# A Fourier mixing layer with a two-layer product on one core: how the first group of rows is normalised, when its mixture is formed, and when five pieces are folded

## The chip, the cores and the metric

One core of a Trainium2 chip runs the whole program. The metric is the device time of one execution in microseconds (us), and the median of three executions stands for the kernel. Five engines work side by side, each through its own list of instructions in order: PE (TensorE, matmuls), DVE (VectorE), ACT (ScalarE), POOL (GpSimd) and SP (SyncE), which here issues nearly all DMA transfers. An engine that waits for a semaphore holds up everything behind it in its own list.

## What is computed

Input x has 8 batches of 3136 positions and 256 channels.

```python
X = np.fft.rfft(x, axis=1)
y = np.fft.irfft(X * F, n=3136, axis=1)              # F: complex filter, per frequency and channel
mixed = np.real(np.fft.fft(np.fft.fft(y, axis=1), axis=2))
u = y + mixed
un = (u - mean(u)) / np.sqrt(var(u) + 1e-06)         # over the channels
out = u + np.maximum(un @ w_ch1, 0.0) @ w_ch2        # 256 -> 1024 -> 256
```

## The kernel before, in words

**The work.** The forward transform of a batch is two matmul passes (`forward1`, `forward2`), with the filter applied in `spectrum`. From the filtered spectrum two things are made. `inverse1` and `inverse2` give y; between the two the data makes a trip through DRAM (`d2`, stored at L689 and loaded at L736), and y itself goes to DRAM as `dy`. `fold` gives the spectrum's even and odd parts, in seven pieces of 224 slots per batch, as an fp16 high half and a low half in `eo`: POOL adds (L633, L646), ACT writes the high half (L662), DVE the low half (L664). A piece of batch 0 is scaled by `first`, which needs the largest values of x and of the filter (`scale_first`, `prepare_filters`, `pow2`).

**The groups.** The 12544 rows are taken in 49 groups of 256 slots (two tiles of 128). For a group, `prepare` forms the mixture on PE from `eo` (`channels`, L890), adds y to it on DVE (L900), takes mean and variance (L957, L958), the root on ACT (L964), normalises on ACT (L984), splits in fp16 halves (L987 ACT, L999 POOL), and transposes by DMA (L1004). Group 0 differs: y comes straight from `direct` (L763) and was copied from PSUM by ACT (L766), the low half is made by DVE and the transpose is done on PE (`flip`, L313). `first_product` makes for each of eight slices `h_0` to `h_7` six matmuls (L1028), a relu on ACT (L1038) and the low half on DVE (L1039); `second_product` makes twelve matmuls per slice (L1058) and at the end adds on DVE (L1067) and stores.

**Weights.** w1 and w2 come as 64-bit words. `widen` (four DVE operations L1078 to L1084 and one on ACT, L1082) makes fp32 of each quarter, `squares` finds the largest column, `bound_weights` the scale, `split_weights` the fp16 halves (L1153 ACT, L1140 DVE).

**What sets the order.** The main program is a list of steps written by hand: `advance` steps the forward side, `give` steps the way back, `weigh` the weights by tables of step numbers (`WIDEN_AT`, `SQUARE_AT`, `BOUND_AT`). A scheduler then places instructions on each engine, with `after(...)` as further constraints, so the order on an engine is known only from the built program. `warm` puts matmuls on PE whose result nothing reads ("idle" in the rows).

**Batch 1** begins with loads of x (`x_0` to `x_6`, L449), seven squares on ACT (`xsq`, L455), the scale `sx`, and then its first pass (`s_1_0` and on, L479), whose table `s1f` is loaded on SP's queue at L477 behind the transposes L1004.

```python
for _ in range(AHEAD):
    next(work, None)               # group 1 begins ahead of the product loop
...
warm(34, "i1", p=idle[0])          # L678
...
if b == 0 and c < 8:
    warm(6, "i2", p=idle[0])       # L809, behind each of y_2 to y_7
```

## Time and profile before

| | |
|---|---|
| median of 3 executions | 1445.79 us (1441.25 to 1446.78) |
| the profiled execution, its own time | 1446.62 us |
| span of the profiled execution | 1444.8 us |
| busy: PE, DVE, ACT, POOL | 1403.2 (97%), 1045.3 (72%), 757.8 (52%), 507.4 (35%) us |
| the two products, L1058 and L1028 | 592.7 and 581.4 us busy on PE |
| chain that ended last, shares by engine | PE 64%, DVE 12%, DMA 10%, issue 6% |
| granted TensorE clock, mean | 0.996 |

How to read it: the span runs from the first to the last instruction, and the 1.8 us between it and the execution's time lie around it. Busy shares are averages over the whole span. In the rows further down a line of a timeline gives start, duration, engine, line, operation, output and inputs, shapes, how many were merged, and in brackets the idle time ahead of it with what ended it. Merged or neighbouring instructions overlap a little, so the step from one to the next is often 0.05 to 0.1 us shorter than the duration of one.

### The profile page before, as it was taken

What the parts mean: (1) busy time and instruction counts of PE and PEld (TensorE: products, weight loads), DVE (VectorE), ACT (ScalarE), POOL (GpSimd) and SP (SyncE); (2) the same over time, 40 slices, a digit from 0 to 9 for tenths busy, and PEclk for the clock granted to TensorE, in tenths of its full rate; (3) what the DMA queues carried; (4) which work ended last, traced back from release to release, by engine and by line L of the source; (5) the groups of instructions that cost most, each with busy time, mean ns of one, the idle gap of its engine ahead of it and who ended that gap; (6) DMA issues with size and microseconds to landing.
All of it is one profiled execution on the core that took longest, in us unless ns stands there. A gap on an engine that the chain in (4) does not pass through costs nothing.

```text
span 1444.8 us, 30052 instructions
## 1 busy us (share of the span) xinstructions
PE 1403.2 (97%) x11292; PEld 948.3 (66%) x11292; DVE 1045.3 (72%) x2326; ACT 757.8 (52%) x1418; POOL 507.4 (35%) x641
## 2 busy tenths in 40 slices
PE   9988999899999999999999999999999999999998
PEld 8745676467666676666766776666766667666666
DVE  7885793679797777978678876987768876545553
ACT  6666455546465554745546554565447564444341
POOL 2521581068103840157300871048400673011010
PEclk9999999999999999999999999999999999999999
DMA  9667888689857967589566987589575987452320
GB/s 361 228 210 204 220 193 243 191 219 227 262 153 184 230 175 245 162 205 226 155 225 178 242 193 208 157 233 245 137 257 155 222 191 196 109 156 80 88 59 29
DMA packets 434221, 276.42 MB, mean 191 GB/s; under 512 B 218796, under 2 KB 401084, under 8 KB 434076
## 3 DMA queue, kind: packets, MB, share of 16 engines
q1 hardware_dynamic: 433948, 274.47, 70.4%
q8 instruction: 88, 1.44, 0.4%
q14 instruction: 57, 0.47, 0.1%
q10 hardware_dynamic: 128, 0.05, 0.0%
HBM read 124.41 MB, written 99.17 MB: 155 GB/s over the span
## 4 chain that ended last, share of the span: by engine, by line
PE 64%; DVE 12%; DMA 10%; issue 6%; ACT 3%; POOL 3%; SPq 2%; DVEq 0%; ACTq 0%; POOLq 0%
PE h L1028 24%; PE acc L1058 23%; DMA x<-x 2%; PE y L801 2%; DVE y L900 2%; PE s L493 2%; DMA at<-d 2%; PE mix L890 2%; DVE h L1039 2%; DMA d<-ast 2%; PE s L479 1%; PE s L590 1%; PE i L684 1%; PE i L686 1%; PE i L685 1%
## 5 line engine op out<-in xcount | busy, mean ns | idle before, releaser
L1028 PE MATMUL h<-ut,home 128*128 128x512 f16 x2352 | 581.4, 380 | 15.2 <-DVE h L1039 7.6
L1058 PE MATMUL acc<-w2s,h 128*128 128x256 f16 x4704 | 592.7, 273 | 2.4 <-DVE y L1067 1.4
L1058 PEld LDWEIGHTS <-h 128*128 128x128 f16 x4704 | 455.5, 98 | 146.3 <-issue 16.4
L1038 ACT ACTIVATE h<-h 128x512 f16<-128x512 f32 x392 | 233.2, 596 | 374.0 <-PE h L1028 364.9
L1039 DVE SCALAR_TENSOR_TENSOR h<-h,h 128x512 f16<-128x512 f32 x392 | 267.8, 685 | 212.5 <-ACT h L1038 211.4
L1028 PEld LDWEIGHTS <-home 128*128 128x128 f16 x2352 | 221.6, 98 | 226.1 <-issue 37.5
L999 POOL TENSOR_TENSOR u<-un,u 128x512 f16<-128x512 f32 x96 | 110.8, 1171 | 674.7 <-ACT u L987 616.1
L900 DVE SCALAR_TENSOR_TENSOR y<-mix,alpha,y 128x508 f32<-128x508 f32 (+1 forms) x368 | 155.9, 476 | 2.1 <-PE mix L890 1.0
L984 ACT ACTIVATE un<-y,sb 128x256 f32<-128x256 f32 x194 | 101.0, 592 | 39.4 <-DVE sb L973 34.4
L607 POOL TENSOR_TENSOR yt<-yt,t 128x224 f32<-128x224 f32 x108 | 75.6, 700 | 119.5 <-DVE t L599 58.7
L812 ACT ACTIVATE ys<-y,alpha 128x512 f32<-128x512 f32 x98 | 66.7, 687 | 61.3 <-PE y L801 60.8
L688 DVE TENSOR_TENSOR bt<-i,bt 112x512 f16<-112x512 f32 x98 | 66.3, 684 | 43.9 <-ACT bt L687 40.9
L1067 DVE SCALAR_TENSOR_TENSOR y<-acc,beta,y 128x512 f32<-128x512 f32 x98 | 71.0, 745 | 25.8 <-PE acc L1058 25.7
L633 POOL TENSOR_TENSOR ef<-yt 128x224 f32<-128x224 f32 x112 | 73.0, 672 | 35.0 <-PE utt L313 17.5
L621 POOL TENSOR_TENSOR home<-yt,home 128x448 f16<-128x448 f32 x77 | 79.5, 1036 | 11.6 <-ACT home L620 11.5
L595 DVE SCALAR_TENSOR_TENSOR yt<-s,pF,ft 128x448 f32<-128x448 f32 x98 | 66.0, 675 | 24.2 <-PE s L591 17.5
L687 ACT CAST bt<-i 112x512 f16<-112x512 f32 x98 | 56.8, 584 | 48.6 <-PE i L686 42.4
L608 POOL TENSOR_TENSOR yt<-yt,t 128x224 f32<-128x224 f32 x108 | 73.1, 679 | 0.0
L957 DVE BATCH_NORM_STATS2 st<-y 128x6 f32<-128x256 f32 x196 | 72.9, 411 | 0.2
L306 DVE TENSOR_REDUCE mx<-x 112x1 f32<-112x1024 f32 x42 | 51.0, 1215 | 25.6 <-DMA x<-x 25.4
L599 DVE SCALAR_TENSOR_TENSOR t<-s,pF,ft 128x448 f32<-128x448 f32 x98 | 66.1, 675 | 0.6 <-POOL yt L608 0.6
L659 POOL TENSOR_TENSOR eo<-ef,eo 128x448 f16<-128x448 f32 (+6 forms) x55 | 51.6, 942 | 33.8 <-ACT eo L658 32.4
(168 smaller groups left out, 1662.0 us busy)
## 6 DMA issues: line engine op xcount, KB each, us to landing
x<-x SPq DMA_DIRECT2D x55, 512.0 KB
out<-y SPq DMA_DIRECT2D x98, 256.0 KB
at<-d SPq DMA_DIRECT2D x49, 512.0 KB
b<-d SPq DMA_DIRECT2D x49, 512.0 KB
dy<-ys SPq DMA_DIRECT2D x206, 112.0 KB
y<-dy SPq DMA_DIRECT2D x90, 256.0 KB
d<-ast SPq DMA_DIRECT2D x98, 224.0 KB
d<-bt SPq DMA_DIRECT2D x98, 224.0 KB
```

Source lines behind the costliest of these rows:

```text
L607: nc.gpsimd.tensor_tensor(yh[:, 0], yh[:, 0], t2v[:, 1], op=ALU.subtract)
L608: marks["sum"] = nc.gpsimd.tensor_tensor(yh[:, 1], yh[:, 1], t2v[:, 0], op=ALU.add).ins
L621: nc.gpsimd.tensor_tensor(ylo, ytv, yhi, op=ALU.subtract)
L633: nc.gpsimd.tensor_tensor(ef[:, i], yt[:, 0, i], yt[:, 1, i], op=o)
L900: nc.vector.scalar_tensor_tensor(out, p, al, y, op0=ALU.mult, op1=ALU.add)
L957: nc.vector.bn_stats(st[:m, 2 * t + k], y[:m, t, k])
L984: nc.scalar.activation(un[:m, k], y[:m, t, k], AF.Identity, bias=sb[:m, i, 1:2], scale=sb[:m, i, 3:4])
L999: marks["u16", g] = low.tensor_tensor(u16[:m, :, :, 1], unv, u16[:m, :, :, 0], op=ALU.subtract).ins
L1028: marks["pe"] = nc.tensor.matmul(p[:, c0 : c0 + n].rearrange("p (t k q) -> p t k q", k=2, q=m), homes["w1s"][:, d, hw, 128 * f : 128 * f + ...
L1038: marks["relu"] = nc.scalar.activation(h[:, 0, :nt], p[:, :nt], AF.Relu).ins
L1039: marks["h"] = nc.vector.scalar_tensor_tensor(h[:, 1, :nt], p[:, :nt], 0.0, h[:, 0, :nt], op0=ALU.max, op1=ALU.subtract).ins
L1058: nc.tensor.matmul(acc[:m, k], h[:, hh, c0 : c0 + m], w2s[:, f, hw], start=f == 0 and k == 0 and i == 0, stop=f == 7 and k == 1 and i == 2,)
```

## The change

Five things change together.

1. **Scales.** `scale_x` finds the scale of x at step 20 instead of with the filter's at step 50; the filter's squares move from steps 42 to 48 to steps 36 to 42, and `scale_first` to step 49. `first` is formed ahead of `set_alpha`, and the small ACT operation for `fnyqs` goes behind group 0.
2. **Mixture of group 0.** `mixture(0)` is issued ahead of `inverse2`'s first step, so on PE it stands ahead of `direct`. ACT copies it from PSUM to two SBUF tiles, `near` and `point`.
3. **Group 0 by tiles.** `prepare_first` adds y from `direct`'s PSUM bank (`sums[t]`) and takes roots, scales and normalisation per tile. The copy L766 of y is gone.
4. **Folds.** Pieces 0 and 1 of batch 0 are folded as before. Pieces 2 to 6 are folded behind group 0 (`late_fold`), pieces 2 and 3 ahead of the loop, the others at its steps 4 to 6. Their `ef` tiles take buffers of tag `t2`. Group 1's `prepare` is begun inside the loop's first step.
5. **Weights and warming.** Squares are spread over steps 44 to 68, w2's split is started at the loop's step 0 instead of 2, w2's scale is found in group 0's time (step 70 instead of 1001), and `warm` shrinks from 34 to 18 and from 6 to 4.

```diff
-WIDEN_AT = (31, 33, 37, 41, 54, 54, 56, 56)
-SQUARE_AT = (56, 70)
-BOUND_AT = (57, 1001)
+WIDEN_AT = (31, 33, 37, 41, 50, 51, 61, 61)
+SQUARE_AT = (44, 46, 56, 56, 68, 68, 68, 68)
+BOUND_AT = (57, 70)
...
-    def scale_first():
+    def scale_x():
...
         pow2(mx0[:, 7:8], "x0", sx, spare)
         sxs[0] = sx
+
+    def scale_first():
         prepare_filters()
+        marks["first"] = nc.vector.tensor_tensor(first, sxs[0][:, 1:2], pF[:, 1:2], op=ALU.mult).ins
         set_alpha(0)
-        nc.vector.tensor_tensor(first, sx[:, 1:2], pF[:, 1:2], op=ALU.mult)
...
-                    with after("utt", "w2s", "relu"):
+                    with after("utt", "w2s", "relu", ("cast", 1)):
                         nc.scalar.activation(junk, x, AF.Square, accum_out=m[:, k : k + 1])
...
-                        with after("spread" if ch < 4 else "utt"):
+                        with after("spread", "utt", "w2s"):
                             nc.scalar.activation(hi, e, AF.Copy, scale=first)
-                        with after(("u16", 0)):
+                        with after("utc", "w2l"):
                             nc.vector.scalar_tensor_tensor(lo, e, first, hi, op0=ALU.mult, op1=ALU.subtract)
...
-                    warm(34, "i1", p=idle[0])
+                    warm(18, "i1", ("pb", "F"), p=idle[0])
...
-        for ch in range(7) if b == 0 else ():
-            fold(ch)
-            yield
+        if b == 0:
+            for ch in range(2):
+                fold(ch)
+                yield
+            folded.extend(range(2, 7))
+            fold_of.append(fold)
...
-            marks["y0"] = nc.scalar.copy(ys_of[0][:, t], p).ins
+            sums[t] = p
...
-                warm(6, "i2", p=idle[0])
+                warm(4, "i2", p=idle[0])
...
+    def prepare_first():
+
+        pm, fix = mixtures.pop(0)
+        near, point = (fp.tile([128, 2, 256], F32, tag="ast", name=n, bufs=4) for n in ("near", "point"))
+        nc.scalar.copy(near, pm)
+        marks["near"] = nc.scalar.copy(point[:1, 0], fix[0][2]).ins
...
+        for t in range(2):
+            add(y[:, t], pm[:, t], al, sums[t])
...
+            moments(0, y, [(t, groups[0][t])], st, mv)
+            roots(sb, mv, [(128, slice(2 * t, 2 * t + 2))])
+            yield
...
-    while done[0] < 60:
+    while done[0] < 58:
...
-        for q in {28: (0, 4), 29: (2,), 30: (6,), 42: (1,), 44: (5,), 46: (3,), 48: (7,)}.get(n, ()):
+        for q in {28: (0, 4), 29: (2,), 30: (6,), 36: (1,), 38: (5,), 40: (3,), 42: (7,)}.get(n, ()):
             measure_filters(q)
-        if n == 50:
+        if n == 20:
+            scale_x()
+        if n == 49:
             scale_first()
...
+    for _ in mixture(0):
+        pass
+    first_group = prepare_first()
+    next(first_group)
...
+    late_fold()
+    late_fold()
...
-        if q == 1:
-            weigh(1001)
-        if 1 < q < 6:
-            split_weights("w2", q - 2)
+        if q == 0:
+            work = prepare(1)
+            for _ in range(AHEAD):
+                next(work, None)
+        if q < 4:
+            split_weights("w2", q)
+        else:
+            late_fold()
```

Where instructions come to stand, at three places.

DVE, from the scaled maximum of the filter to `first`. Before (`lines_F` itself is eleven rows ahead; `cv`, `home` and `y_3` rows are the widening of w2):

```order
L1084 SCALAR_TENSOR_TENSOR home<-size_777,home 128x512
L1079 SCALAR_TENSOR_TENSOR y_3_582<-raw_739,cv_7_834 128x512
L300 TENSOR_REDUCE pF<-pb_F 128x1
L1080 SCALAR_TENSOR_TENSOR home<-raw_663,home 128x512
L1080 SCALAR_TENSOR_TENSOR y_3_582<-raw_739,y_3_582 128x512
L302 TENSOR_SCALAR pF<-pF 128x1
L1084 SCALAR_TENSOR_TENSOR home<-size_831,home 128x512
L1084 SCALAR_TENSOR_TENSOR y_3_582<-size_838,y_3_582 128x512
L303 TENSOR_SCALAR pF<-pF 128x1
L430 TENSOR_TENSOR first<-sx_714,pF 128x1
```

Now, the whole piece from `lines_F`:

```order
L296 TENSOR_SCALAR lines_F<-ident,mF 128x128
L1128 TENSOR_SCALAR cv_4_745<-raw_598 128x512
L647 MEMSET ef_0_818 128x1
L1129 SCALAR_TENSOR_TENSOR home<-raw_598,cv_4_745 128x512
L1130 SCALAR_TENSOR_TENSOR home<-raw_598,home 128x512
L1134 SCALAR_TENSOR_TENSOR home<-size_749,home 128x512
L300 TENSOR_REDUCE pF<-pb_F 128x1
L302 TENSOR_SCALAR pF<-pF 128x1
L303 TENSOR_SCALAR pF<-pF 128x1
L431 TENSOR_TENSOR first<-sx_271,pF 128x1
```

Of the sixteen widening operations for w2 all stood ahead of `first`; now four do.

ACT, in group 0's product (`h_0_4`, `h_0_6` are relus of slices 4 and 6, `un_0` and `un_1` the normalised tiles of group 1 and then of group 2, `u_1_0` a cast of group 1, `sb` a root, `xsq` the squares of batch 1). Before:

```order
L1038 ACTIVATE h_0_4_1289<-h_4_1282 128x512
L1153 ACTIVATE w2s<-home,sw_1216 128x2x256
L455 ACTIVATE xsq_0_1310,mx_1123<-x_0_1116 112x1024
L455 ACTIVATE xsq_1_1313,mx_1123<-x_1_1117 112x1024
L455 ACTIVATE xsq_2_1316,mx_1123<-x_2_1118 112x1024
L984 ACTIVATE un_0_1173<-y_1127,sb_1166 128x256 x2
L984 ACTIVATE un_1_1190<-y_1127,sb_1166 128x256 x2
L814 COPY ys_10_1305<-y_10_1306 112x512
```

Now:

```order
L1088 ACTIVATE h_0_6_1342<-h_6_1335 128x512
L959 ACTIVATE sb_1311<-mv_1309,eps 128x4
L1049 ACTIVATE un_0_1153<-y_1085,sb_1138 128x256 x2
L1049 ACTIVATE un_1_1162<-y_1085,sb_1138 128x256 x2
L1052 CAST u_1_0_1156<-un_0_1153 128x4x128
L1052 CAST u_1_1_1165<-un_1_1162 128x4x128
L457 ACTIVATE xsq_0_1283,mx_1081<-x_0_1074 112x1024
L457 ACTIVATE xsq_1_1286,mx_1081<-x_1_1075 112x1024
L457 ACTIVATE xsq_2_1289,mx_1081<-x_2_1076 112x1024
L1049 ACTIVATE un_0_1397<-y_1173,sb_1311 128x256 x2
L457 ACTIVATE xsq_3_1329,mx_1081<-x_3_1077 112x1024
L1049 ACTIVATE un_1_1447<-y_1173,sb_1311 128x256 x2
```

Group 1's normalisation and all seven squares now stand behind the relu of slice 6 and behind group 2's root (`sb_1311`). The rows that follow are `xsq_4`, `xsq_5`, the cast of group 2's first tile, `xsq_6`, the cast of its second, and the relu of group 1's slice 0.

SP's queue, around the table `s1f` of batch 1 (`ut_1155` and `ut_1336` are the transposes of groups 1 and 2; `ut_1135` and `ut_1308` now). Before:

```order
L1004 DMA_TRANSPOSE ut_1155<-u_1_0_1176 128x8x128
L1004 DMA_TRANSPOSE ut_1155<-u_1_1_1193 128x8x128
L518 DMA s_1243<-c_s 128x896
L477 DMA s1f_1391<-c_s1f 112x112
L518 DMA s_1243<-c_s 128x896
L1004 DMA_TRANSPOSE ut_1336<-u_2_0_1422 128x8x128
```

Now:

```order
L1054 DMA_TRANSPOSE ut_1135<-u_1_0_1156 128x8x128
L1054 DMA_TRANSPOSE ut_1135<-u_1_1_1165 128x8x128
L1054 DMA_TRANSPOSE ut_1308<-u_2_0_1400 128x8x128
L479 DMA s1f_1369<-c_s1f 112x112
L520 DMA s_1207<-c_s 128x896
```

The load of `s1f` now stands behind group 2's first transpose as well. On PE, ahead of `s_1_0` stand now two slices of group 1 (`h_0` and `h_1`) where there was one, and the second of them takes the PSUM bank of the first, so it waits for that slice's low half on DVE.

## Rows read from the trace of the kernel before

**Rows 1.** Windows: stretch, length, busy us of PE, PEld, DVE, ACT, POOL, then clock, DMA share.

```profile
0.00:100.00 100.00, 90.57 (x605) 67.77 (x606) 78.23 (x184) 63.69 (x130) 34.63 (x49) 1.00 0.78 273
...
300.00:1300.00 1000.00, 986.34 (x8229) 665.86 (x8228) 761.54 (x1668) 532.73 (x990) 395.45 (x499) 1.00 0.76 197
```

**Rows 2.** Timeline of DVE, 53 to 67 us.

```profile
53.87 0.84 DVE L605 TENSOR_TENSOR yt<-yt,t 128x224 f32<-128x224 f32 x1
...
58.30 1.29 DVE L1079 SCALAR_TENSOR_TENSOR home<-raw,cv 128x512 int32<-128x512 int32 x2
...
63.79 0.29 DVE L300 TENSOR_REDUCE pF<-pb_F 128x1 f32<-128x128 f32 x1
...
66.52 0.16 DVE L430 TENSOR_TENSOR first<-sx,pF 128x1 f32<-128x1 f32 x1
```

**Rows 3.** Timeline of ACT at 59 us.

```profile
59.15 0.59 ACT L679 COPY bt<-i 112x512 f32<-112x512 f32 x1 [0.28 <-PE i L673]
```

**Rows 4.** Timeline of PE, 62 to 92 us.

```profile
62.20 4.26 PE L283 MATMUL idle<-still 128*128 128x512 bf16 x19
66.30 5.34 PE L763 MATMUL y<-b,direct 112*128 112x256 f32 x24
...
72.59 0.50 PE L890 MATMUL mix<-mix,eo 128*128 128x129 f16 x7
...
76.27 1.02 PE L791 MATMUL y<-b,i2f 112*112 112x512 f32 x2
...
77.13 1.46 PE L283 MATMUL idle<-still 128*128 128x512 bf16 x6
...
90.19 0.94 PE L313 MATMUL utt<-ident,u 128*128 128x128 f16 x14
...
91.94 1.47 PE L1028 MATMUL h<-ut,home 128*128 128x512 f16 x6 [0.59 <-DVE ut L315]
```

**Rows 5.** Timeline of SP's queue, 62 to 88 us.

```profile
62.36 4.14 SPq L736 DMA_DIRECT2D b<-d_f  x6
...
83.42 1.81 SPq L741 DMA_DIRECT2D dy<-ys  x4
...
87.71 0.39 SPq L877 DMA_DIRECT2D y<-dy  x1
```

**Rows 6.** Timeline of DVE, 91 to 111 us.

```profile
91.80 0.74 DVE L900 SCALAR_TENSOR_TENSOR y<-mix,alpha,y 128x508 f32<-128x508 f32 x1
...
92.98 1.64 DVE L900 SCALAR_TENSOR_TENSOR y<-mix,alpha,y 128x254 f32<-128x254 f32 x4
...
110.21 0.30 DVE L958 BATCH_NORM_AGGREGATE mv<-st 128x2 f32<-128x6 f32 x2
```

**Rows 7.** Timeline of ACT, 104 to 116 us, and of POOL at 115.76 us.

```profile
104.81 1.05 ACT L455 ACTIVATE xsq<-x 112x1024 bf16<-112x1024 f32 x1
...
107.94 2.06 ACT L984 ACTIVATE un<-y,sb 128x256 f32<-128x256 f32 x4
...
115.06 0.63 ACT L987 CAST u<-un 128x512 f16<-128x512 f32 x1
...
115.76 2.28 POOL L999 TENSOR_TENSOR u<-un,u 128x512 f16<-128x512 f32 x2 [15.80 <-ACT u L987]
```

**Rows 8.** Timeline of SP's queue, 117 to 122 us, and of PE behind it.

```profile
117.66 2.69 SPq L1004 DMA_TRANSPOSE ut<-u  x2
...
121.09 0.36 SPq L477 DMA_DIRECT2D s1f<-c_s1f  x1
...
123.63 3.66 PE L479 MATMUL s<-x,s1f 112*112 112x512 f32 x8 [0.18 <-DMA s1f<-c_s1f]
```

**Rows 9.** Windows of one microsecond, as Rows 1; then PE's timeline at 290 us.

```profile
120.00:121.00 1.00, 0.00 (x0) 0.00 (x0) 0.41 (x4) 1.00 (x3) 0.00 (x0) 1.00 0.80 184
...
289.00:290.00 1.00, 0.00 (x0) 0.00 (x0) 1.00 (x3) 0.00 (x0) 0.00 (x0) 0.50 0.97 255
...
290.08 4.81 PE L1028 MATMUL h<-ut,home 128*128 128x512 f16 x12 [4.21 <-DMA ut<-u]
```

More of the change, by code (lines that the diff above doesn't have):

```diff
@@ L938, in prepare, with moments @@
             yield
[L939 to L954 removed]
+        mixtures[g] = pm, fix
+    mixtures = {}
+    def moments(g, y, tiles, st, mv):
+        for t, (g0, g1) in tiles:
             m = g1 - g0
@@ new lines, in prepare @@
+    def prepare(g):
+        tiles = groups[g]
+        yield from mixture(g)
+        pm, fix = mixtures.pop(g)
+        y = ys_of.pop(g)
+        for t, s, _, _ in fix:
+            keep = mp.tile([128, 2, 256], F32, tag="un", name=f"keep_{g}", bufs=2)[:, 0]
+            nc.scalar.copy(keep[s], y[s, t, 1])
+        for t, (g0, g1) in enumerate(tiles):
+            ps = slice(0, g1 - g0)
+            with after(("u16", 0)) if g == 1 else after("h"):
+                add(y[ps, t], pm[ps, t], alpha_of(g0, g1, f"al_{g}_{t}")[ps], y[ps, t])
+        for t, s, pn, al in fix:
+            add_nyquist(y[s, t, 1], pn, al[s], keep[s])
+        yield
+        ut = mp.tile([128, 2, 8, 128], F16, tag="ut", name=f"ut_{g}", bufs=2)
+        mv, st, sb = small(g)
+        n = tiles[0][1] - tiles[0][0]
+        nt = 2 * len(tiles)
+        moments(g, y, list(enumerate(tiles)), st, mv)
+        parts = [(n, slice(0, nt))]
+        if len(tiles) == 2 and tiles[1][1] - tiles[1][0] != n:
+            parts = [(n, slice(0, 2)), (tiles[1][1] - tiles[1][0], slice(2, 4))]
+        roots(sb, mv, parts)
+        yield
+        scales(g, sb, mv, parts)
+        yield
+        for t, (g0, g1) in enumerate(tiles):
+            m = g1 - g0
@@ L1114, in widen_weights, with square_weights @@
         else:
-            with after("low"):
+            with after("low", "first" if i > 4 else ""):
                 widen(w, words[i], f"{i}")
-    def square_weights(name):
+    def square_weights(i):
+        name = ("w1", "w2")[i // 4]
         ws, m = raws[name]
-        with after("act", "y0"):
-            for i, w in enumerate(ws):
-                squares(m[:, i : i + 1], w, f"{name}_{i}")
+        with after("act", "spread" if i in (2, 3) else "", "near"):
+            squares(m[:, i % 4 : i % 4 + 1], ws[i % 4], f"{name}_{i % 4}")
     def bound_weights(name):
         ws, m = raws[name]
-        with after(("u16", 0)):
+        with after("low"):
             nc.vector.tensor_reduce(m[:, 4:5], m[:, 0:4], axis=AX.X, op=ALU.max)
@@ L1139, in lower_weights @@
         for lo, w, scale, hi in lows:
-            nc.vector.scalar_tensor_tensor(lo, w, scale, hi, op0=ALU.mult, op1=ALU.subtract)
+            lowered[:] = [nc.vector.scalar_tensor_tensor(lo, w, scale, hi, op0=ALU.mult, op1=ALU.subtract).ins]
         lows.clear()
@@ L1184, in give @@
     def give(n):
-        while come[0] < min(n, NB * BACK) and done[0] >= STEPS * (come[0] // BACK + 1) - (1 if come[0] >= BACK else 4):
+        while come[0] < min(n, NB * BACK) and done[0] >= STEPS * (come[0] // BACK + 1) - (1 if come[0] >= BACK else 5):
             next(home)
@@ L1239, in _program @@
         give(come[0] + 1)
-    for i, _ in enumerate(prepare(0)):
+    for i, _ in enumerate(first_group):
         weigh(68 + i)
         give(min(come[0] + 1, KEPT))
-    with after(("u16", 0)):
-        weigh(1000)
+    weigh(1000)
+    with after("utt"):
+        nc.scalar.activation(fnyqs, fnyq, AF.Copy, scale=pF[:, 1:2])
     advance(STEPS + 3)
@@ L1248, in _program, with late_fold @@
     halves = load_halves()
-    work = prepare(1)
-    for _ in range(AHEAD):
-        next(work, None)
+    def late_fold():
+        if folded:
+            fold_of[0](folded.pop(0))
+    late_fold()
+    late_fold()
     per = NS // 32
```

143 lines of the change are left out of this document (69 added, 74 removed).

## The prediction, as put on record

> **What bounds the kernel now.** I read the page first: PE is busy 97% of the span. The windows then say where its 3% are missing: from 300 to 1300 us PE is busy 986 of 1000 us, in the first 100 us only 91 [rows 1]. The lists of all engines are the same again from batch 3 on and nearly so from 130 us, so all that this change can move lies ahead of 130 us. It reaches the end only if PE passes 130 us earlier or later with the same work behind it. I therefore followed the timelines from 53 to 130 us, at each idle stretch asking what ended it.
>
> Ahead of group 0's product PE waits on a chain: the filter's scale gives `first` at 66.5 [rows 2], then the fold and mixture, y_2 to y_7, the flips, and h_0 at 91.94 [rows 4]. At the far end of group 0, PE is idle at 120 us [rows 9] until group 1's transposed tiles land. Then `s_1_0`, the first pass of batch 1, starts at 123.63, released by the load of `s1f` [rows 8]. The question is whether a lead at 92 us survives to 123.
>
> The sum is made against the profiled execution (1446.62 us, 1.8 of it outside the span), which lies 0.83 us above the median, 1445.79. I subtract the difference from the median. A measurement of this kernel tells about 0.5%, or 7.2 us, from no change.
>
> **Scales and the early mixture.** The last value `lines_F` rests on is ready when yt ends, 53.87 + 0.84 = 54.7 [rows 2], and nothing of x's scale stands ahead of it any more. Of sixteen widening operations four are left ahead of `first`, at 0.6 us each (two step 1.2, [rows 2]): 54.7 + 2.4 = 57.1 for the reduction that was at 63.79, then under 1 us of small operations. `first` is there at about 58.1, 8.4 us earlier.
>
> This does not move `direct` by 8.4 us. It waits for the trip through DRAM: the last copy to `bt` was at 59.15 [rows 3], the loads of `b` began at 62.36 [rows 5], and `direct` at 66.30 stood behind the last of 34 warming matmuls, 62.20 + 4.26 less overlap [rows 4]. I take the copy 0.3 us earlier, the loads at 62.0, and the first tile landed at 65.2 (bounds: 64, by the 62.36 and the 1 to 2 us that six loads of 4.14 us leave for the first, and 66.3, no change). The mixture costs PE the 1.6 us from 71.6 (66.30 + 5.34) to 72.59 + 0.50 [rows 4]. It moves into the trip, where PE had only warming work, so I cost it at nothing. Its cover: the two high halves, about the 0.6 of a `bt` copy each [rows 3], end near 62, the low halves 0.6 later, the matmuls at 64. If the trip were shorter than that, its 1.6 us would be back ahead of `direct`. The two copies `near` and `point` stand where the copy L766 stood.
>
> **From `direct` to h_0.** `direct` ends at 65.2 + 5.3 = 70.5. y_2 to y_7 cost PE 0.86 each (76.27 to 77.13) and six warms stepped 1.3 us, 0.216 each [rows 4]; with four it is 6 x (0.86 + 0.86) = 10.4, to 80.9. `pb_w` of w2's scale stands behind y_7 on PE, and DVE's reduction of it stands ahead of group 0's low halves, so these come at 81.6 to 82.9. From the last flips to h_0 it was 90.19 to 91.94, or 1.75 us. h_0 at 84.6, **7.3 us earlier**. Of this the 28 warms left out are 28 x 0.216 = 6.0 us. The y halves that DVE adds straight from PSUM and the root taken per tile lie beside y_2 to y_7 and cost nothing there.
>
> **Where the lead goes.** Behind slice 6's relu ACT's list now holds group 2's root, then group 1's normalisation. The root waits for DVE's `mv` of group 2. DVE's list up to there took 91.80 to 110.5 [rows 6], 18.7 us. Now two low halves of folds, two of slices and one of w2s join it, 5 x 0.6 = 3.0 (at a widening operation's price), and 2.0 go, my estimate for the small operations of w2's scale (0.15 to 0.3 each) and half a us idle. It starts at 86.7 (group 1's first add, 5.1 us earlier rather than 7.3 because ACT first copies `ut` and three y and writes the next fold's half). 86.7 + 18.7 + 3.0 - 2.0 = 106.4; the root ends at 106.7.
>
> ACT then runs a closed row [rows 7]: four `un` 2.0, two casts 1.1, three squares 3.1, two `un` 1.0, a square 1.05, two `un` 1.0, two squares 2.1, a cast 0.5: 118.5. POOL's low half takes 1.14 (119.6), SP's transpose about 1.25 (120.9), and `s1f` now stands behind this transpose on SP's queue. From its issue to `s_1_0` it was 121.09 to 123.63, 2.54 us [rows 8]: **`s_1_0` at 123.5, where it was 123.63.** The lead is gone, apart from one slice more that PE has behind it, 1.4 us.
>
> PE's idle time shows where. Group 1's first tiles are cast at 109.2; low half and transposes (117.66 to 122.0, the h ahead of `s_1_0` [rows 8]) put its h_0 at 115. Group 0's work is used up at 109 to 111. Its h_1 shares the PSUM bank and waits for h_0's low half, whose relu stands behind the last square and cast on ACT (120.1): 121.3. So PE is idle from about 110 to 115 and from 116.4 to 121.3.
>
> **The clock.** In the idle microsecond at 120 the granted clock was 1.00; in the one at 289, late in an idle time of 4.21 us, it was 0.50, and the twelve matmuls behind it took 4.81 us where six take 1.47 [rows 4, 9]. So a stretch at the lower level cost about 1.9 us there. The new idle stretches are as long as the one at 290, so I take a drop, at 1.2 us, since part of the slow slice ends before `s1f` lands (bounds: 0 and 1.9). [...]
>
> **Sum:** -1.4 + 1.2 = -0.2 us: 1445.79 - 0.2 = **1445.6 us**. The forecast's own range is 1442.5 to 1448.5: the landing of `b` and the estimates on DVE and ACT give 1 to 2 us either way, the clock 0.7 up and 1.2 down.
>
> **Edits that I cost at nothing.** Folds 2 to 6 leave ACT and DVE ahead of h_0 and stand beside group 0's product; their cover is PE's own work on group 0, from h_0 to the idle time before 120 us, and they are late only for group 1's mixtures (their low halves are among the 3.0 above). w2's split comes two steps earlier; its one operation ahead of group 2's root is among the 3.0 too. w2's squares lie in ACT's gaps while PE is at y_2 to y_7.
>
> **Rivals.**
> *A. The lead is kept whole.* If group 2's `mv` is ready much earlier than 106 us, as when the DVE list is shorter than I count, ACT's row starts at once and `s1f` lands by 116. Then 1445.8 - 7.3 = 1438.5. For it: the squares stood ahead of the normalisation before (104.81 against 107.94, [rows 7]) and the first transposes would come early. Against: the order puts group 2's root ahead of group 1's `un`. Chance 0.10.
> *A2. Part is kept,* 2 to 6 us, about 1442: some of DVE's 18.7 us were waits, or the queue lets `s1f` go earlier. Chance 0.13.
> *B. Slower: y of group 1 comes late.* Its second fetch waits for stores of ys, and the copy of ys_4 stands now behind that of `ut` on ACT (about 85). First store to fetch was 83.42 to 87.71, 4.3 us [rows 5]: issue at 89.2. Before, its landing came no later than the second tile's first add, the last of the four at 92.98, which ends at 94.6 and takes 0.74, so at 93.9 [rows 6]: at most 6.2 us. It would land by 95.4 at the worst, and DVE wants it at 92.1. It decides if it lands after 92.1, that is over 2.9 us from its issue. DVE then stands 3.3 us, group 2's fetch behind three loads of x up to 2 us more, and everything down the closed row moves with it: -1.4 + 3.4 + 2.1 = +4.1, 1449.9. For it: DVE and ACT have no slack from 87 to 120. Against: the transfer is small and 6.2 is only a bound. [...] Chance 0.10.
> *C. The change does not do what it says:* the mixture or y_7 is late and h_0 comes less than 3 us earlier. Then ACT's closed row starts up to 4 us later, and the time is about 1448. Chance 0.05.
>
> **How the numbers follow.** Forecast 0.62, A 0.10, A2 0.13, B 0.10, C 0.05. Faster by over 0.5% (below 1438.6) is A: 0.10. Slower by over 0.5% (above 1453.0) is half of B, with a clock drop more, and a little of C: 0.06. The rest, 0.84, is within it. The range reaches from A, 1438.5, to B's price and a clock drop of 1.6, 1451.5; what B and C have beyond, and what lies below A, is under 2 in 10.
>
> **What would show it.** Right: the reduction of pF at 57 and `first` at 58; the mixture's matmuls ahead of `direct`; h_0 near 84.6; root of group 2 on ACT near 106.7 behind DVE's `mv`; PE idle near 110 to 115 (ended by `ut`) and 116 to 121 (ended by the low half of h); `s_1_0` near 123.5 to 124 behind `s1f`; a granted clock of 0.50 about there; no difference behind 300 us. Wrong: `s_1_0` before 118 (A), an idle DVE at 92 to 95 behind a DMA of y (B), or h_0 after 89 (C).

## The result and the profile after

The change made the kernel **slower**: 1458.45 us, the median of 9 runs (1454.63 to 1460.74), against 1446.78 us (1441.25 to 1451.68) for the kernel before in the same session. The ratio is 1.0072, with an interval of 1.0051 to 1.0092. The forecast was 1445.6 us in a range of 1438.5 to 1451.5, so the range did not hold the time, and the outcome that got a chance of 0.06 came true. A repetition (experiment 5) gave 1.0086.

The profiled execution took 1458.59 us, its span 1456.8. The busy line of the page has the same work in more time:

```profile
PE 1404.8 (96%) x11264; PEld 950.4 (65%) x11264; DVE 1046.5 (72%) x2330; ACT 758.5 (52%) x1419; POOL 508.6 (35%) x641
```

PE is busy 1.6 us longer than before with 28 matmuls less, and idle 10.4 us longer. The windows (stretch, length, busy us of PE, PEld, DVE, ACT, POOL, clock, DMA share) say where; the last line is the kernel before:

```profile
0.00:100.00 100.00, 89.39 (x568) 68.93 (x569) 75.45 (x174) 62.92 (x130) 32.94 (x45) 0.95 0.71 250
70.00:75.00 5.00, 3.43 (x8) 2.83 (x9) 2.88 (x8) 4.14 (x11) 0.00 (x0) 0.57 1.02 344
120.00:130.00 10.00, 2.72 (x6) 0.89 (x7) 0.18 (x2) 10.00 (x22) 2.57 (x3) 0.60 0.25 61
300.00:1300.00 1000.00, 981.70 (x8230) 662.19 (x8229) 763.14 (x1675) 534.16 (x993) 393.71 (x498) 1.00 0.75 197
345.00:500.00 155.00, 145.53 (x1206) 97.89 (x1205) 122.85 (x265) 80.94 (x152) 54.71 (x68) 0.99 0.79 203
...
345.00:500.00 155.00, 151.63 (x1254) 101.94 (x1253) 125.06 (x276) 84.30 (x159) 59.04 (x75) 1.00 0.81 209
```

The first and the fourth line answer to [rows 1]. The second and the third show two places with a lower clock, at 70 and at 120 us (a third, at 46 us, is told in experiment 5). The forecast had "no difference behind 300 us". There is one: 4.6 us of PE's busy time are missing there (986.34 to 981.70). Between 345 and 500 us alone it is 6.1 (151.63 to 145.53), so all of it is lost there, and a little comes back elsewhere.

PE's timeline from 60 us to batch 1 (start, duration, engine, line, operation, output and inputs, in brackets the idle time ahead and what ended it) answers to [rows 4] and [rows 8]:

```profile
60.15 0.22 PE L299 MATMUL pb_F<-lines_F,still 128*128 128x128 bf16 x1 [0.62 <-DVE lines_F L296]
...
62.11 4.05 PE L283 MATMUL idle<-still 128*128 128x512 bf16 x18
66.80 0.29 PE L896 MATMUL mix<-mix,eo 128*128 128x129 f16 x2 [0.64 <-ACT eo L664]
...
71.57 8.37 PE L768 MATMUL y<-b,direct 112*128 112x256 f32 x24 [2.94 <-issue]
79.78 1.02 PE L796 MATMUL y<-b,i2f 112*112 112x512 f32 x2
...
90.13 0.22 PE L299 MATMUL pb_w<-lines_w,still 128*128 128x128 bf16 x1
...
93.53 1.47 PE L1078 MATMUL h<-ut,home 128*128 128x512 f16 x6 [0.79 <-DVE ut L315]
...
124.24 2.72 PE L1078 MATMUL h<-ut,home 128*128 128x512 f16 x6 [5.97 <-DMA ut<-u]
130.72 2.72 PE L1078 MATMUL h<-ut,home 128*128 128x512 f16 x6 [3.77 <-DVE h L1089]
133.33 4.76 PE L481 MATMUL s<-x,s1f 112*112 112x512 f32 x8
```

The mixture stands ahead of `direct`, as the change says. But `direct` starts at 71.57 instead of 66.30 and takes 8.37 us instead of 5.34: the same 24 matmuls, most of them at the lower clock (granted 0.50 from 71 to 77.5). h_0 comes at 93.53, 1.6 us **later** than before, and `s_1_0` at 133.33, 9.7 later. In the repetition h_0 comes at 91.58, a little earlier than before, and `s_1_0` at 132.98 all the same.

Why `direct` is late stands in ACT's timeline. Before, the last copy to `bt` began at 59.15 [rows 3]:

```profile
59.17 0.59 ACT L681 COPY bt<-i 112x512 f32<-112x512 f32 x1 [0.28 <-PE i L675]
...
63.33 0.67 ACT L1132 ACTIVATE size<-raw 128x512 f32<-128x512 f32 x1 [3.08 <-DVE home L1134]
63.90 1.05 ACT L681 COPY bt<-i 112x512 f32<-112x512 f32 x2
```

In the kernel before the next `size` stood behind the last copy, and waited there without harm:

```profile
62.10 0.68 ACT L1082 ACTIVATE size<-raw 128x512 f32<-128x512 f32 x1 [2.36 <-DVE home L1084]
```

In the change `size`, an operation of w2's widening, stands in ACT's list ahead of the last two copies. It waits 3.08 us for DVE, and the copies wait behind it and end at 64.95 (PE's sums for them were done at about 62.2). SP's queue then carries that on ([rows 5] had 62.36):

```profile
67.83 2.60 SPq L743 DMA_DIRECT2D b<-d_f  x5
```

From that issue to `direct` it is 3.74 us; before it was 3.94. And DVE, for which `size` waits, is itself late:

```profile
57.41 0.85 DVE L607 TENSOR_TENSOR yt<-yt,t 128x224 f32<-128x224 f32 x1
58.18 1.92 DVE L296 TENSOR_SCALAR lines_F<-ident,mF 128x128 bf16<-128x128 f32 x1
...
61.19 1.03 DVE L1130 SCALAR_TENSOR_TENSOR home<-raw,home 128x512 int32<-128x512 int32 x1
62.26 1.03 DVE L1134 SCALAR_TENSOR_TENSOR home<-size,home 128x512 f32<-128x512 f32 x1
...
63.79 0.15 DVE L431 TENSOR_TENSOR first<-sx,pF 128x1 f32<-128x1 f32 x1
```

`yt` ends at 58.3 where [rows 2] had 54.7; `lines_F` takes 1.92 us (0.287 in the trace of before), and `pb_F`, which waits for it, now stands on PE ahead of the last eight matmuls that these copies need (PE idles 0.62 us there, above); `first` comes at 63.79, 2.7 us earlier instead of the 8.4 forecast. POOL's timeline has its folds at the same time:

```profile
57.97 0.80 POOL L648 TENSOR_TENSOR ef<-yt 1x224 f32<-1x224 f32 x1
58.74 1.27 POOL L635 TENSOR_TENSOR ef<-yt 128x224 f32<-128x224 f32 x2
```

They end at 60.01, and `lines_F` at 60.10.

Behind h_0 the closed row on ACT is there. Its root starts at 115.82 behind DVE, and the four `un` of group 1 follow:

```profile
115.82 0.30 ACT L959 ACTIVATE sb<-mv,eps 128x4 f32<-128x4 f32 x1 [1.71 <-DVE sb L968]
```

### The profile page after: what moved, and what is told of

Same layout as the page of the kernel before. It is cut to its first block, busy times and chain, and to the rows that moved or that the text cites. A ratio compares the mean times of both kernels' runs of the same rounds, so it can differ in the third digit from the quotient of the medians.

```text
span 1456.8 us, 29996 instructions
## 1 busy us (share of the span) xinstructions
PE 1404.8 (96%) x11264; PEld 950.4 (65%) x11264; DVE 1046.5 (72%) x2330; ACT 758.5 (52%) x1419; POOL 508.6 (35%) x641
## 4 chain that ended last, share of the span: by engine, by line
PE 74%; DMA 9%; issue 5%; DVE 5%; POOL 4%; ACT 2%; SPq 1%; DVEq 0%; POOLq 0%; ACTq 0%
PE h L1078 28%; PE acc L1108 27%; PE s L495 3%; PE y L806 3%; PE mix L896 2%; DMA x<-x 1%; PE i L686 1%; PE s L481 1%; DMA b<-d 1%; DMA at<-d 1%; PE i L688 1%; PE i L687 1%; PE s L592 1%; DMA dy<-ys 1%; PE s L593 1%
## 5 line engine op out<-in xcount | busy, mean ns | idle before, releaser
L1078 PE MATMUL h<-ut,home 128*128 128x512 f16 x2352 | 585.0, 382 | 23.9 <-DMA ut<-u 12.4
L906 DVE SCALAR_TENSOR_TENSOR y<-mix,alpha,y 128x508 f32<-128x508 f32 (+1 forms) x360 | 152.6, 475 | 5.6 <-PE mix L896 4.5
L690 DVE TENSOR_TENSOR bt<-i,bt 112x512 f16<-112x512 f32 x98 | 66.3, 683 | 39.3 <-ACT bt L689 35.0
```

Source lines behind the costliest of these rows:

```text
L906: nc.vector.scalar_tensor_tensor(out, p, al, y, op0=ALU.mult, op1=ALU.add)
L1078: marks["pe"] = nc.tensor.matmul(p[:, c0 : c0 + n].rearrange("p (t k q) -> p t k q", k=2, q=m), homes["w1s"][:, d, hw, 128 * f : 128 * f + ...
```

## Experiments

Each was timed against the kernel before on the same chip, in several executions except where the text says otherwise. Medians of the kernel before lay between 1447.58 and 1448.8 us.

**1. `size` behind the copies of bt.** One edit to the changed kernel:

```diff
-        nc.scalar.activation(size, high.bitcast(F32), AF.Abs)
+        with after("spread" if name in ("6", "7") else ""):
+            nc.scalar.activation(size, high.bitcast(F32), AF.Abs)
```

> Edit: the ACT operation `size` of w2's last two quarters is kept behind the last copy to bt; nothing else of the change differs. Theory T1 (the late start of group 0 comes from ACT: `size` stands ahead of the last two copies to bt and waits for a DVE operation that ends at 63.3, so the trip through DRAM starts about 2.2 us late, PE idles 2.9 us ahead of direct and runs it at the lower clock): last copy to bt ends near 62.5 instead of 64.95, direct starts near 69.4 instead of 71.57 and takes 5.3 us instead of 8.4, h_0 near 88.3 instead of 93.53, and since the back of group 0 only passes it on, s_1_0 near 128 instead of 133.3; time about 1453. Rival R1 (the trip is late because its matmuls are late and DMA is slow, ACT's order does not matter): direct moves by under 0.5 us, time 1458 as the change.

1449.4 us, ratio 1.0014 (0.9996 to 1.0031). The timeline, rows of ACT, SP's queue and PE:

```profile
61.62 0.58 ACT L681 COPY bt<-i 112x512 f32<-112x512 f32 x1 [0.28 <-PE i L675]
...
64.94 3.98 SPq L743 DMA_DIRECT2D b<-d_f  x6
...
68.66 5.42 PE L768 MATMUL y<-b,direct 112*128 112x256 f32 x24 [0.90 <-PE pb_w L299]
...
129.59 5.20 PE L481 MATMUL s<-x,s1f 112*112 112x512 f32 x8
```

The copies wait for PE alone now, `direct` starts 2.9 us earlier than in the profile above (1.7 than in the repetition), PE idles 0.90 us ahead of it, and `direct` takes 5.42 us at full clock (granted 1.00 from 70 to 75). h_0 comes at 87.99, as expected, `s_1_0` 3.7 us earlier than in the change. The edit brings back some 10 of the 11.7 us, more than the theory had priced; but not all of that is the place of `size`, since this program also has another order on all engines from about 145 to 460 us (behind experiment 12).

**2. 34 warms again.** The loads stay late; only PE's idle time ahead of `direct` is filled.

```diff
-                    warm(18, "i1", ("pb", "F"), p=idle[0])
+                    warm(34, "i1", ("pb", "F"), p=idle[0])
```

> Edit: 34 warming matmuls behind the last inverse pass instead of 18; nothing else differs. T1 (direct takes 8.4 us because PE stood idle for 2.9 us and ran at the lower of its two clocks): PE has warming work until about 69.4, granted clock 1.00 from 70 to 78, direct starts near 71.6 as before and takes 5.3 us, h_0 near 90.5, time about 1455.5. Rival R1: direct is slow for another reason (its operands or weights land late); it still takes 8 us and the time stays 1458.

1448.05 us, ratio 1.0005 (0.999 to 1.0019). PE's timeline:

```profile
69.77 5.42 PE L768 MATMUL y<-b,direct 112*128 112x256 f32 x24 [0.55 <-PE mix L896]
```

and the window from 70 to 75 us, as above:

```profile
70.00:75.00 5.00, 5.00 (x24) 4.40 (x24) 4.49 (x12) 4.54 (x12) 0.00 (x0) 1.00 1.01 342
```

`direct` starts only 0.5 us earlier than in the repetition of the change (experiment 5) and still ends 2.8 earlier; h_0 comes at 87.73 against 91.58. So 16 warming matmuls, 16 x 0.216 = 3.5 us of PE's otherwise idle time, kept the clock at 1.00; leaving them out saved nothing and cost 2.8 us at the end of `direct`. `s_1_0` comes at 127.55. The time fell by 11 us where about 3 were expected; here too the order differs, from about 305 to 460 us.

**3. The squares of x early.** In the change they wait for a cast of group 1, which puts them into ACT's closed row. Here that wait is dropped; the late `direct` stays.

```diff
-                    with after("utt", "w2s", "relu", ("cast", 1)):
+                    with after("utt", "w2s", "relu"):
```

> Edit: batch 1's seven squares no longer wait for group 1's casts on ACT; nothing else differs. In this order the load of s1f stands ahead of all transposes on SP's queue, and s_1_0 ahead of group 1's h_0 on PE. Theory T2 (the lead of group 0 is lost behind it, because squares, group 1's and group 2's normalisation form one closed row on ACT and s1f stands behind its end): h_0 of group 0 stays at 93.5, s_1_0 moves from 133.3 to about 118 to 121, PE has no idle stretch over 3 us from 118 to 133 and keeps its clock, time 1446 to 1449. Rival R2 (group 1's tiles are what PE lacks, the squares only fill ACT's idle time): s_1_0 starts no earlier than 129, gain 4 us at most, time 1454 or more.

1445.5 us, ratio 0.9984 (0.9968 to 1.0). `direct` is as bad as in the change (69.78, for 8.52 us) and h_0 at 91.90, yet:

```profile
120.01 6.21 PE L481 MATMUL s<-x,s1f 112*112 112x512 f32 x10 [1.04 <-DMA s1f<-c_s1f]
```

`s_1_0` comes 13 us earlier than in the change from about the same h_0: with the squares the load of `s1f` and `s_1_0` itself move ahead of group 1's products. Behind 160 us this program has the order of the kernel before.

**4. Experiments 1 and 3 together** (both edits as above).

> Edit: both of the two edits, `size` behind the copies to bt and the squares without their wait for group 1's casts. T1 and T2 together: h_0 of group 0 near 88.3, s_1_0 at 113 to 117, time 1440 to 1444, below the kernel before. Rival R3 (the two are not additive, since with s1f early PE waits next for group 1's transposes or for DVE): time 1445 to 1448, as with the squares alone.

1442.94 us, ratio 0.9967 (0.9947 to 0.9986): faster than the kernel before. h_0 at 87.17, `s_1_0` at 115.11. At `s_1_0` the two gains add up (3.7 and 13.3 us alone, 18.2 together). In time they do not: against the repetition of the change they are 9.7 and 13.6 us alone and 16.1 together.

**5. The change once more**, unedited.

> The change itself once more, on the chip and beside the runs of the other kernels of this set, to have its time under the same conditions. T1 and T2: direct at the lower clock in the profile again (over 8 us), h_0 6 to 10 us later than the 84.6 that was forecast, s_1_0 later than 130; time 1455 to 1460. Rival R4 (the first measurement was off by the chip it ran on): time within 3 us of the kernel before.

1459.07 us, ratio 1.0086 (1.0067 to 1.0104). PE's timeline:

```profile
70.31 7.67 PE L768 MATMUL y<-b,direct 112*128 112x256 f32 x24 [2.93 <-issue]
```

and the same window:

```profile
70.00:75.00 5.00, 4.69 (x11) 3.81 (x12) 1.64 (x5) 3.78 (x8) 0.00 (x0) 0.51 0.98 315
```

`s_1_0` is at 132.98 here. Executions differ a little already at 44 us. PE's transposes there, in the kernel before, the profile of the result, this execution and experiment 1:

```profile
43.31 0.65 PE L542 MATMUL at<-ident,xc 128*112 128x128 f32 x4 [0.48 <-ACT at L549]
...
44.16 0.65 PE L544 MATMUL at<-ident,xc 128*112 128x128 f32 x4 [0.48 <-ACT at L551]
...
44.39 0.65 PE L544 MATMUL at<-ident,xc 128*112 128x128 f32 x4 [0.48 <-ACT at L551]
...
44.97 0.65 PE L544 MATMUL at<-ident,xc 128*112 128x128 f32 x4 [0.48 <-ACT at L551]
```

From there to `direct` it is 23.0, 27.4, 25.9 and 23.7 us. The profile of the result had a lower clock at 46 us (0.84 from 40 to 50), which put `direct` 1.5 us later; this execution has not, and the time is the same.

**6. `lines_F` on ACT**, one execution. In experiment 5, as in the change, `lines_F` took 1.92 us on DVE while POOL was in its folds; is it slow of itself, or only there? In the second case the author's estimate was that `direct` would start 1 to 1.5 us earlier. The edit leaves out the floor of 1e-18 for the filter's lines.

```diff
-        nc.vector.tensor_scalar(lines, ident[:rows, :rows], col, 1e-18, op0=ALU.mult, op1=ALU.max)
+        if name == "F":
+            nc.scalar.activation(lines, ident[:rows, :rows], AF.Copy, scale=col)
+        else:
+            nc.vector.tensor_scalar(lines, ident[:rows, :rows], col, 1e-18, op0=ALU.mult, op1=ALU.max)
```

> Edit: the one operation lines_F (the diagonal matrix from the filter's largest value) runs on ACT instead of DVE; its lower bound of 1e-18 is left out. Nothing else of the change differs. [...] Rival R5 (lines_F is slow of itself, or waits for mF): it is as slow on ACT, or its place in time does not change.

1455.37 us, which lies among the times of the change. The timeline, rows of ACT, DVE and POOL:

```profile
55.39 0.40 ACT L297 ACTIVATE lines_F<-ident,mF 128x128 bf16<-128x128 f32 x1
...
56.35 2.12 DVE L1131 TENSOR_SCALAR cv<-raw 128x512 int32<-128x512 int32 x1
...
56.92 1.27 POOL L638 TENSOR_TENSOR ef<-yt 128x224 f32<-128x224 f32 x2
...
61.88 0.42 DVE L1131 TENSOR_SCALAR cv<-raw 128x512 int32<-128x512 int32 x1
```

`lines_F` is quick, but the next operation on DVE now takes 2.12 us, where the same one takes 0.42 later, and ends 0.3 after POOL's folds. The wait moved to another operation; `direct` came 0.3 us earlier once 0.57 are taken off by which this execution ran ahead already at 46 us. That fits POOL's folds as the cause, but the 1 to 1.5 us of the estimate were not there.

**7. The kernel before with the change's warms** (34 to 18 and 6 to 4), nothing else of the change.

> The kernel before with one part of the change alone: 18 warming matmuls instead of 34 and 4 instead of 6. T1 (direct waits for the landing of b, 3.7 us behind the first load at 62.4, and idle time ahead of it costs the clock): direct starts at 66.1 as before, PE idles 2.5 to 4 us ahead of it, and if the granted clock falls direct takes 8 us; y_2 to y_7 save 2.6 us; h_0 between 91 and 94, time within 3 us of the kernel before. Rival R6 (my count: every warming matmul left out is 0.216 us gained): h_0 near 86, lead kept in part, time 1443 to 1446 where the kernel before has 1448.

1448.35 us, ratio 1.0005 (0.999 to 1.0021). PE's timeline:

```profile
67.28 7.11 PE L763 MATMUL y<-b,direct 112*128 112x256 f32 x24 [3.20 <-ACT fnyqs L354]
...
96.31 1.47 PE L1028 MATMUL h<-ut,home 128*128 128x512 f16 x6 [1.32 <-DVE ut L315]
```

With 28 matmuls less h_0 comes 4.4 us **later** than [rows 4]; 1.1 of that this execution was late already at 44 us (44.37), so the matmuls left out make 3.3. `direct` loses its clock about one us in, behind 3.2 us of idle time (granted 0.83 from 65 to 70 and 0.82 from 70 to 75). h_0 is later than the 91 to 94 that were expected. `s_1_0` follows by 3.2 (126.81), the time hardly at all.

**8. Experiment 4, and `s1f` in a buffer of its own**, loaded once and early.

```diff
-                    table = fp.tile([112, 112], F32, tag="x16", name=f"s1f_{b}", bufs=3)
-                    nc.sync.dma_start(table, a["c_s1f"])
+                    if "s1f" not in tables:
+                        tables["s1f"] = cp.tile([112, 112], F32, name="s1f_own")
+                        nc.sync.dma_start(tables["s1f"], a["c_s1f"])
+                    table = tables["s1f"]
```

> The two edits of the fourth run, and s1f has a buffer of its own, so that its load waits for no square. Theory T2 carried on (behind group 0, s_1_0 waits for s1f, whose buffer a square holds until the last part of x lands): s_1_0 starts with the end of group 0's products, near 112 instead of 115.1, PE's idle time of 2.5 us and the lower clock behind it are gone, time 2 to 4 us below the fourth run, 1439 to 1441. Rival R7 (the copies of s_1_0 on ACT need the scale of the last square anyway, PSUM is full after a few products): PE stops after a few matmuls of s_1 until about 117, gain under 1 us.

1441.4 us, ratio 0.9961 (0.9947 to 0.9976), the fastest of all. PE's timeline:

```profile
114.11 0.21 PE L299 MATMUL pb_x<-lines_x,still 112*128 112x112 bf16 x1 [2.28 <-DVE lines_x L296]
114.16 4.50 PE L483 MATMUL s<-x,s1f_own 112*112 112x512 f32 x10
```

Without the load, `s_1_0` waits for DVE's scale of x, and so comes only 1 us earlier than in experiment 4, less than expected. Whether this beats experiment 4 is open: the intervals overlap.

**9. One warm more** (18 to 19), meant to change the scheduler's lists far behind it and nothing that the theories speak of.

> Edit: 19 warming matmuls instead of 18 in the change, nothing else. On PE that is 0.2 us of work in idle time, so by the chip alone it should change nothing. But the scheduler, which places instructions by its own model of time, makes other choices behind it: up to the relu of group 0's slice 5 the lists are those of the change but for a few neighbours, from about 140 us they differ, and they come back to those of the kernel before at about group 9, where the change's own come back at group 11. Theory T4 (of the change's loss some 3 to 5 us arise behind 150 us, from lists of the engines that differ from those of the kernel before, in waits of PE between 340 and 500 us): h_0 and s_1_0 at about the times of the change (91.6 and 133 within 1 us, direct at the lower clock), and yet time 1453 to 1456. Rival R8 (all of it is lost by 133 us and what follows only wanders from execution to execution): time 1457 to 1460, as the change.

1459.25 us, ratio 1.0066 (1.0042 to 1.0091). The expectation took it that the lists differ from about 140 us. The traces show that they do not: ACT, SP and POOL run theirs in the order of the change, PE and DVE with a few neighbours changed ahead of 92 us. So this is the change's order timed once more, with the same time, and it does not tell whether that order costs part of the 12 us.

**10. Group 2's root behind group 1's casts.** It stood at the head of ACT's closed row.

```diff
-        roots(sb, mv, parts)
+        with after(("cast", 1)) if g == 2 else nullcontext():
+            roots(sb, mv, parts)
```

> Edit: the root of group 2 on ACT is queued behind group 1's casts; the squares keep their wait for those casts. Theory T2 (closed row on ACT, in which group 1's normalisation waits for group 2's variance): group 1's un starts behind the relu of slice 6, about 2 us earlier than in the change, group 1's h_0 about 2 us earlier; the load of s1f now stands ahead of group 2's transposes on SP's queue, but its buffer waits for squares, so s_1_0 starts near 128 to 130 instead of 133; by this 1455, and 1450 to 1453 if its other lists behind 150 us are better as well. Rival R9 (the squares alone close the row): group 1's h_0 and s_1_0 within 1 us of the change, time 1457 to 1460.

1455.49 us, ratio 1.0045 (1.003 to 1.0059). Group 1's first product and `s_1_0`:

```profile
122.32 2.72 PE L1079 MATMUL h<-ut,home 128*128 128x512 f16 x6 [5.89 <-DMA ut<-u]
...
130.56 3.85 PE L481 MATMUL s<-x,s1f 112*112 112x512 f32 x8
```

A gain of 3.6 us, to 1455 as expected. Group 1's first product comes 1.9 us earlier and `s_1_0` 2.8: the root's wait is a small part of the row, the squares (experiment 3) the large one. Behind about 300 us this program too has another order than the change.

**11. The kernel before, delayed**: 44 warms more behind y_7, so that h_0 is late; the rest of the text of the program is unchanged.

```diff
-                warm(6, "i2", p=idle[0])
+                warm(50 if c == 7 else 6, "i2", p=idle[0])
```

> The kernel before, with 44 warming matmuls more behind y_7 on PE (9.5 us of work that nothing reads), nothing else: group 0's product begins 9.5 us later, with no idle time of PE ahead of it. It measures what a late group 0 costs at the end of the kernel. Theory T5 (the end follows the start of batch 1's first pass: what is late there by 9 us is late at the end by 9 us or a little more): h_0 near 101.4, s_1_0 near 131 to 133, time 1456 to 1459 where the kernel before has 1448. Rival R10 (what follows has slack, in its waits for DMA at 206 and 290 us, and takes up a part): s_1_0 as late, but time 1451 to 1454; then the change loses the rest elsewhere, behind 133 us.

1453.52 us, ratio 1.0032 (1.0018 to 1.0047). h_0 comes 9.2 us later (101.17), `s_1_0` 4.4 later (128.06), and the time is 5.2 above the kernel before. About half of h_0's lateness is absorbed on the way to batch 1. The time came out as the rival had it, at 1453.5. That the 4.4 us at `s_1_0` and the 5.2 at the end are close does not mean that the delay was passed on, as the table behind experiment 12 shows.

**12. The same with 68 warms more** (`50` is `74`), to see whether a start of batch 1 at 133 us alone makes the loss between 345 and 500 us.

> The kernel before, with 68 warming matmuls more behind y_7 instead of 44 (nothing else of the change). In the profiles so far PE's busy time between 345 and 500 us is 151.0 to 153.2 us where s_1_0 comes at or before 129.6 us, 149.9 where it comes at 130.6, and 145.5 to 146.3 where it comes at 131.5 or later (all three of these with the change's lists). 24 warms more put h_0 at about 106.4 and s_1_0 at about 133.2. T9 (lateness alone: a start of batch 1 behind 131 us uses up the slack of the waits at 350 and 408 us, whatever the lists): PE's busy time in 345 to 500 falls to 145 to 148 us, and the time is 1458 to 1463 us. R9 (those waits are the change's own, by its order of work up to 480 us): the busy time there stays at 150 to 153 us, and the time is 1455.5 to 1458 us, the 4.4 to 5.2 us that s_1_0 comes later than in the shorter delay added to its 1453.5.

1456.77 us, ratio 1.005 (1.0037 to 1.0064), with `s_1_0` at 132.87. The windows, first of this kernel:

```profile
345.00:500.00 155.00, 154.18 (x1269) 104.07 (x1268) 124.62 (x273) 84.18 (x158) 58.16 (x72) 1.00 0.77 207
```

and of experiment 9, with `s_1_0` at 131.55:

```profile
345.00:500.00 155.00, 146.11 (x1218) 97.93 (x1215) 124.42 (x272) 82.31 (x154) 56.89 (x72) 1.00 0.79 203
```

At the same lateness PE loses nothing there in this kernel: lateness alone does not make these waits. They go with the order of work. PE's busy time there is 145.5 to 146.9 us in the change and experiments 5, 6 and 9, which share the change's order, and 149.85 us or more in all others. No run has the change's order with an early `s_1_0`, so whether the order makes the waits without a late start is not shown. What ended the idle time there was, in the change's groups of PE's instructions by line:

```profile
L686 PE MATMUL i<-z,i 112*112 112x256 f16 x22 | 6.4, 291 | 4.5 <-DMA z<-home 3.0 <-DMA z<-y 1.6
L1078 PE MATMUL h<-ut,home 128*128 128x512 f16 x246 | 62.2, 384 | 4.0 <-DVE h L1089 2.0 <-DMA ut<-u 2.0
```

**The order of work, and what becomes of a delay.** A trace holds the instructions of each engine in the order in which they ran, so the orders of two kernels can be compared. One edited operation moves the scheduler's choices far behind it. The change's order differs from that of the kernel before up to about 445 us; experiments 1, 2 and 10, apart from the edit itself, leave the change's order at 145 to 305 us and are back at the old one, but for a neighbour or two, by about 380; experiments 7, 11 and 12 differ from the kernel before up to about 375 as well. The table follows the matmuls of the first product (`h`<-`ut`,`home`), 2352 in every kernel, in the profiled executions: how many us later than in the kernel before the matmul comes that stood there at 270, 453 and 674 us, and the last one.

| kernel | `s_1_0` later by | at 270 | at 453 | at 674 | last |
|---|---|---|---|---|---|
| change | 9.7 | 7.8 | 13.2 | 12.7 | 11.8 |
| 5, the same | 9.4 | 8.1 | 12.4 | 12.7 | 12.7 |
| 9, the same order | 7.9 | 5.9 | 10.3 | 9.6 | 10.8 |
| 6, the same order | 8.0 | 4.8 | 7.8 | 7.5 | 8.6 |
| 10, another order | 6.9 | 5.7 | 7.9 | 6.6 | 7.3 |
| 1, another order | 6.0 | 7.0 | 4.7 | 5.3 | 6.3 |
| 2, another order | 3.9 | 2.7 | 3.0 | 0.7 | 0.2 |
| 7, before, fewer warms | 3.2 | 4.0 | 1.2 | 0.9 | 2.7 |
| 11, before, delayed | 4.4 | 2.8 | 1.0 | 0.6 | 8.2 |
| 12, before, delayed more | 9.2 | 8.2 | 5.7 | 2.5 | 12.8 |

With the change's order a delay grows by 3 to 5 us between 270 and 453 us. With the orders of experiments 1, 7, 11 and 12 it shrinks there by 2 to 3, and with that of 10 it grows by 2. And a late batch 1 is not what 11 and 12 end with: at 674 us they are 0.6 and 2.5 us late, and the rest comes behind that, for a part between 950 and 1100 us (the kernel before, then experiment 12), where the order is the old one; why is open.

```profile
950.00:1100.00 150.00, 147.70 (x1266) 100.43 (x1265) 115.12 (x248) 76.91 (x142) 63.77 (x81) 1.00 0.79 205
...
950.00:1100.00 150.00, 142.99 (x1205) 96.86 (x1204) 106.90 (x232) 71.36 (x134) 64.13 (x82) 0.97 0.77 202
```

## Why the prediction was wrong, point by point

The steps of the sum, beside the profile of the change:

| step | forecast | measured |
|---|---|---|
| `first` | 58.1 | 63.8 |
| last copy to `bt` ends | 59.4 | 64.95 |
| loads of `b` issued | 62.0 | 67.8 |
| `direct` starts | 65.2 | 71.6 |
| `direct` to y_2 | 5.3 | 8.2 |
| y_2 to y_7 | 10.4 | 10.3 |
| y_7 to h_0 | 3.7 | 3.4 |
| h_0 | 84.6 | 93.5 |
| h_0 to group 2's root | 21.8 | 22.3 |
| root to `s_1_0` | 17.1 | 17.5 |
| `s_1_0` | 123.5 | 133.3 |

- **The step that failed** is "I take the copy 0.3 us earlier, the loads at 62.0, and the first tile landed at 65.2". Of its bounds, 64 and 66.3, the upper one was "no change"; a later trip was not among them. The change moves the widening of w2, and with it `size` into ACT's list ahead of two copies of the trip, where it waits for DVE. I counted DVE's widening operations ahead of `first` and did not ask what ACT's list holds ahead of the copies. Of the 8.9 us by which h_0 misses the forecast, 6.4 are this start. By the distances from 44 us (experiment 5) 2.2 of the 6.4 are `size`, which experiment 1 shows by undoing it (25.9 to 23.7). The others are 1.1 that were forecast as a gain and did not come, 0.7 that stay in experiment 1, 0.9 by which the profiled execution was late at 44 us already, and 1.5 of the lower clock at 46 us, which the repetition had not.
- **"It moves into the trip, where PE had only warming work, so I cost it at nothing."** The mixture did fit into the trip. But the warming work that covered the rest was gone with it, and with the trip longer PE stood idle 2.94 us and `direct` ran mostly at the lower clock: 2.9 of the 8.9 us, and experiment 2 gives them back by filling the gap. The prediction asked about the clock at 120 us and not at 70. "Of this the 28 warms left out are 28 x 0.216 = 6.0 us" fails with it: by itself, in the kernel before, leaving them out makes h_0 3.3 us later (experiment 7).
- **"54.7 + 2.4 = 57.1"** for `first` took DVE's durations from a place where POOL did not fold (it was idle from 55.5 to 69.3 us there). `yt`, which stands ahead of `lines_F` in DVE's list, ended 3.6 us later than I read it, and `lines_F` took 1.92 us instead of 0.287. Through `first` this costs nothing: the mixture was done before `b` landed. It reaches `direct` by another way, through the wait of `size` for DVE and that of `pb_F`.
- **Right**: the closed row. Both of its terms are within 0.5 us, the idle stretches came where they were forecast relative to h_0, ended by `ut` and by the low half of h, with a clock of 0.50 between them. The second term has luck in it: `s_1_0` did not wait for `s1f` but stood behind h_1's six matmuls at the lower clock (2.72 us, 1.47 at the full one). The clock term of 1.2 us was too small: 1.25 there and 1.1 in `s_1_0`'s first eight matmuls (4.76 us for 3.66 in [rows 8]). Against the kernel before this row is nearly all that makes `s_1_0` late: from h_0 to `s_1_0` it was 31.7 us, 38.9 were forecast, 39.8 came (41.4 in the repetition). The forecast had the lead of h_0 pay for that, and there was no lead. Experiment 3 shows that the squares in this row, which the prediction counted but took from the order as given, decide `s_1_0`.
- **The premise** "the lists of all engines are the same again from batch 3 on and nearly so from 130 us" was wrong in part: the change's order differs up to about 445 us, and late as it is it loses 5 to 6 us more between 345 and 500 where experiment 12, as late at `s_1_0`, loses none. From `s_1_0` to the end the loss grows from 9.7 to 12.0 us and not to 15: about 2 us come back ahead of 270 us and about 1 behind 453 (the table).
- **The rivals.** C, an h_0 that gains less than 3 us, is what happened, beyond its price: C had the closed row start up to 4 us later than forecast, at 1448 us, and it started 9.4 later (115.8 for 106.4). B did not come about: no wait of DVE for group 1's y.

What stays open: what a late batch 1 costs at the end by itself. In experiments 1, 2 and 7 `s_1_0` comes 3.2 to 6.0 us later than before and the time only 0 to 1.4, in 11 it comes 4.4 later and the time 5.2; but no two of these kernels have the same order behind 130 us, so the runs do not part the start of batch 1 from the order. That `size`, the warms and the squares make h_0 and `s_1_0` late is shown; how the 11.7 us at the end divide between them and the order behind 300 us is not.

## What to carry to other kernels

When a change moves work into another stretch, read in the new order what every engine's list holds ahead of the hand-over you rely on, and what that work waits for; here `size`, an operation of 0.67 us, waited 3.08 us for DVE, and two copies whose sums PE had done at about 62.2 began behind it at 63.90. Warming work is to be left out only where what follows it is known to be on time: here a gap of 2.94 us opened in its place, and `direct` behind it took 8.37 us, mostly at a granted clock of 0.50, where behind gaps of 0.90 and 0.55 us it took 5.42 at 1.00. And a lead or a delay counts only where it reaches the next stage's start, so look for what else stands in that row (here the squares of x, worth 13 us at `s_1_0`) before shortening what leads up to it. Where a scheduler places the instructions, an edit of one line is an edit of everything behind it: compare the orders in two traces before giving a difference in time to the line.
